# A linear-attention and two-MoE kernel: weight conversions at other places, early weights four chunks ahead, first-step splits moved

## The chip, the core and the metric

One core of one Trainium2 chip. The metric is the device time of one execution in microseconds, median of several runs; the kernel before takes 1228.31 us.

## The reference

The input is attention data (4 batches, 8 heads, 576 positions, head size 64), the probabilities of four experts, and the weights of two feed-forward layers:

```python
q_s = softmax(q, over the 64 columns);  k_s = softmax(k, over the 576 positions)
x = q_s @ (k_s^T @ v)                       # per head; reshaped to 2304 x 512
p = domain_probs / sum(domain_probs)
out = sum over e of p[:, e] * (relu(x @ w1[e]) @ w2[e])     # 4 experts, 512 -> 1024 -> 512
h = out @ w_in;  g = where(h > 0, h, exp(min(h, 0)) - 1)    # 512 -> 2048
return g @ w_out                                            # 2048 -> 512
```

`w_in` and `w_out` come as 64-bit floats; all else is 32-bit.

## The kernel before

**Numbers as pairs.** Each matrix product is done in a fast 32-bit format with a high and a low part: ACT copies the high part, VectorE or GpSimd subtracts it to get the low part, and TensorE does three matmuls (high-high, high-low, low-high). "Splitting" below is that copy and that subtraction.

**Stages.** First comes attention for the sixteen head pairs; the first four (`NPAIR`) are worked off in an order written out by hand (`START`), the others are woven into the next stage. Then comes unit 0, the first expert, in plain form: eight weight chunks `f` (`FPU`), over eight blocks of tokens. `wload` (L403) loads a chunk of both layers into one of two staging buffers `r`, `whi` (L410) and `wlo` (L418) split it; in the first block `wadvance` (L482) splits chunk f+2 after chunk f's first layer, and `wlo_ahead` (L487) starts the next load, since the staging buffer is free then. At the start two chunks are loaded (L527 and `early_loads`, L530).

The rest runs in 30 steps (`STEPS`): ten groups `s` of four chunks by three blocks `b` of 768 tokens. Each step multiplies its first layer with a Strassen scheme: seven products per pair of chunks, two pairs, 14 products (`product`, L1111 is its matmul), with sums in PSUM by VectorE (L1320, L1327) and copies by ACT (L1313, L1315). Steps of s below 5 (`S_FAST`), 15 of them, are "fast": their second layer is a Strassen scheme too (`second_product`, L1255), run during the next step; the intermediate values go through the tile `gt`. In later steps the second layer is plain (`chunk`, L1168 to L1170). Groups s = 0 to 5 belong to experts 2 to 4, s = 6 to 9 (`S_MOE` = 6) to the last layer pair, whose activation needs three ACT functions and two VectorE instructions (`elu`, L1141 to L1146) and a GpSimd subtraction (L1151). Between them the result of the experts is transposed and stored (`turn_steps`, L910 to L965).

**Weights of a step.** `w1_steps` (L714) makes the Strassen sums and splits of the first layer: `sums1` (L746, two subtractions and additions on VectorE, L748 and L749), `sums2` on GpSimd (L753, L754), and splits in between (L733, L744). `w2_fast` (L784) does the same for the second layer of a fast step: `w2_parts` (L769) splits on ACT (L773) and GpSimd (L774), `w2_sum` (L777) is a VectorE subtraction in place (L782).

**Conversions.** No engine computes in 64 bits, so `convert_load` (L428) loads 128 x 512 values of `w_in` or `w_out` as pairs of words (512 KB), `convert` (L440) puts a 32-bit float together in seven instructions (VectorE L455, L461, L465, ACT L468, VectorE L471, L474, and a store to DRAM on SyncE, L477). There are 32 of them, `s // 2` the chunk, `s % 2` the layer; `w_load` (L692) reads the results back from `scratch`. An "aside" conversion uses `gt` for its input and its result (result `y` is L452's slice); the others use the small tiles `ek` and `y`. The result is written first by L461.

**What sets the order.** Each engine and each queue does its work in program order; SyncE (SP) issues nearly all DMAs, one after another, and waits at each until its data and its place are ready. Work that is not TensorE's is hung on hooks: `at(n, fn)` in the first part, one hook per 2048 matmul columns; `at2(i, k, fn)` in the steps, 24 (`SH`) hooks per step, which count on through all steps. A step lets its hooks go at the ends of some products, in batches:

```python
PLAIN, MIXED = ({1: 4, 3: 8, 5: 12, 8: 16, 10: 20, 12: 24}, {      # L1282: after product 1 hooks 0-3, ...
    0: 2, 1: 4, 2: 6, 3: 7, 4: 9, 5: 10, 6: 13, 7: 14, 8: 16, 9: 17, 10: 19, 11: 20, 12: 23, 13: 24,
})
```

`MIXED` holds where the step before was fast, `PLAIN` in the first step and after the fast ones (there `chunk` lets one hook go at a time as well). A conversion is given a hook `t`: its load goes out at t - 7, its six instructions at t + 0, 1, 2, 3, 4, 5 and its store at t + 9 (at 0, 2, 4, 6, 10, 12 and 17 in the fast steps and the first three). The table of hooks is `CONV` (L833 to L837): eight asides in unit 0, thirteen in the fast steps 26 hooks apart, three asides at the end of the fast steps (12 hooks apart, `end1` = 360), eight asides from `end2` (432) + 40 on, again 12 apart.

Of the kernel before, what the change touches and what calls it, by code (L numbers as in the profile page):

```python
# [8 lines left out]
F32 = mybir.dt.float32  # L9
# [12 lines left out]
def tile_attention_moe_moe(  # L22
# [13 lines left out]
    nc = tc.nc  # L36
    NP_, CP, NC, P = q.shape
    D, S = P // 2, NC * CP
    NT, DM = out.shape
    E = w1.shape[0]  # L40
    F2 = w_out.shape[0]
    NPAIR = DM // P
    HALF = S // 2
    KD = DM // P
# [37 lines left out]
    S_MOE = (E - 1) * FPU // FS  # L82
# [22 lines left out]
    stg = ctx.enter_context(tc.tile_pool(name="stg", bufs=2))  # L105
    hp_ = ctx.enter_context(tc.tile_pool(name="hp", bufs=1))
    kvp = ctx.enter_context(tc.tile_pool(name="kvp", bufs=1))
    tmp = ctx.enter_context(tc.tile_pool(name="tmp", bufs=1))
# [18 lines left out]
    gt = hp_.tile([P, 4, TB], F32, name="gt")  # L127
# [273 lines left out]
    raw = {}  # L401

    def wload(u, f):  # L403
        a, b_, _ = units[u]
        r = stg.tile([P, 2, DM], F32, tag="r", name="r")
        nc.sync.dma_start(out=r[:, 0, :].rearrange("p (d f) -> p d f", d=KD), in_=a[f])
        nc.sync.dma_start(out=r[:, 1, :], in_=b_[f * P : (f + 1) * P, :])
        raw[u, f] = (r[:, 0, :].rearrange("p (d f) -> p d f", d=KD), r[:, 1, :])

    def whi(u, f):  # L410
        r1, r2 = raw[u, f]
# [6 lines left out]
    def wlo(u, f):  # L418
        engines = (nc.gpsimd, nc.vector if u == 0 else nc.gpsimd)
        for t, r, eng in zip((w1t[u, f], w2t[u, f]), raw.pop((u, f)), engines):  # L420
            eng.tensor_tensor(out=t[:, 1], in0=r, in1=t[:, 0].bitcast(F32), op=ALU.subtract)  # L421
# [55 lines left out]
        yield lambda: nc.sync.dma_start(out=scratch[s // 2, :, s % 2, :], in_=t["y"])  # L477

    wseq = [(0, f) for f in range(FPU)]
    wnext = [2]  # L480

    def wadvance(u, f):  # L482

        whi(u, f)
        wlo_ahead(u, f)

    def wlo_ahead(u, f):  # L487
        wlo(u, f)
        if wnext[0] < len(wseq):
            wload(*wseq[wnext[0]])  # L490
            wnext[0] += 1

# [26 lines left out]
    t = bank("o")  # L519
# [10 lines left out]
    def early_loads():  # L530
        load(NPAIR - 1, "v")
        wload(*wseq[1])
        for i in range(NPAIR):
            load(i, "q", NC // 2, NC)


    timed = {}

    def at(n, fn):
        timed.setdefault(n, []).append(fn)  # L540
# [41 lines left out]
    for i in range(NP_):  # L582
        late = i >= NPAIR
        t = K_START[i - NPAIR] if late else HALF_STEP * i
        kt = plan_k(i, t) if late else None
        qt = plan_q(i, t + Q_LATE if late else t, kt["kvlo"] if late else 0)
        done.append(qt["xlo"])
        assert qt["xlo"] <= 24 * (i // NPAIR * S // 256 + (not late)) - 2, (i, qt)
        if late:
            for n, when in kt.items():  # L590
                at(when, lambda fn=K_STEPS[n], i=i: fn(i, in_m))
        for n, fn in Q_STEPS.items():
            at(qt[n], lambda fn=fn, i=i: fn(i, in_m, (0, 1) if i >= NPAIR else (1,)))
        if late:
            if i < NPAIR + 2:
                at(i - NPAIR, lambda i=i: load(i, "knqv" if i == NPAIR else "kqv"))
            if i + 2 < NP_:
                at(kt["kv"], lambda i=i: load(i + 2, "kv"))
            if i + 1 < NP_:
                at(kt["kv"], lambda i=i: load(i + 1, "n"))  # L600
            if i + 2 < NP_:
                at(qt["qturn"], lambda i=i: load(i + 2, "q"))
# [111 lines left out]
    def w1_steps(s, p):  # L714

        r, t = [], []
# [23 lines left out]
        tt = nc.vector.tensor_tensor  # L740
# [4 lines left out]

        def sums1():  # L746
            f1, f2 = r[0][:, 0], r[0][:, 1]
            tt(out=f1[:, :2], in0=f1[:, :2], in1=f2[:, :2], op=ALU.subtract)  # L748
            tt(out=f2[:, :2], in0=f2[:, :2], in1=f2[:, 2:], op=ALU.add)  # L749

# [33 lines left out]
    def w2_fast(i, s, d):  # L784

        for k, fn, op in (
            (8, w2_parts, "B11"), (13, w2_sum, "T1"), (17, w2_parts, "T1"), (18, w2_parts, "B22"), (19, w2_sum, "T3"),
            (21, w2_parts, "B21"), (22, w2_parts, "T3"), (24, w2_sum, "T2"), (26, w2_parts, "T2"), (27, w2_sum, "T4"),
            (30, w2_parts, "T4"),
        ):  # L790
            at2(i, k - d, lambda fn=fn, op=op: fn(s, op))

    def w2_step(s, p):
        r = w2r.pop((s, p))
# [11 lines left out]
    def at2(i, k, fn):  # L806
        timed2.setdefault(i * SH + k, []).append(fn)
# [6 lines left out]
    for b in range(NB):  # L814
        need = min(NP_, -(-2 * TB * (b + 1) // S) * NPAIR)
        t = 66 + 36 * b
# [8 lines left out]
        at(n, fn)  # L825
    at(202, lambda: w_load(0, 0, 1))
    at(203, lambda: w_load(0, 1, 1))
    w2_fast(0, 0, 7)

    NCONV = 2 * F2 // P  # L830
    later = lambda n, fn: at2(0, n, fn)
    end1 = NB * S_FAST * SH
    CONV = [(at, t, 1 + (t < 100), True) for t in (30, 50, 70, 146, 160, 173, 185, 197)]  # L833
    CONV += [(later, 34 + 26 * n, 2, False) for n in range(13)]
    CONV += [(later, end1 + 13 + 12 * n, 1, True) for n in range(3)]
    end2 = NB * S_MOE * SH
    CONV += [(later, end2 + 40 + 12 * n, 1, True) for n in range(NCONV - len(CONV))]  # L837
    for s, (put, t, d, aside) in enumerate(CONV):
        put(t - 7, lambda s=s, x=aside: convert_load(s, x))
        for n, fn in zip((0, 1, 2, 3, 4, 5, 9) if d == 1 else (0, 2, 4, 6, 10, 12, 17), convert(s, aside)):  # L840
            put(t + n, fn)
    for i, (s, b) in enumerate(STEPS):
        more = s + 1 < len(STEPS) // NB
# [119 lines left out]
    for b in range(NB):  # L963
        i = NB * (S_MOE - 1) + b + 1
# [79 lines left out]
    for step in START.split():  # L1044
        n, i = step[:-1], int(step[-1])
# [376 lines left out]
```

## Time and profile before

| | us |
|---|---|
| runs: median (lowest to highest) of 3 | 1228.31 (1226.82 to 1230.87) |
| the profiled execution, its own time | 1231.21 |
| its span, first to last instruction | 1229.4 |
| TensorE busy | 1193.3 (97%) |
| VectorE, ACT, GpSimd busy | 826.9, 635.2, 572.8 (67%, 52%, 47%) |
| mean granted clock, as a share of full | 0.989 |

The profile is one execution. PE is TensorE, DVE is VectorE, POOL is GpSimd, SP is SyncE; L followed by a number is a line of the kernel. A row of a timeline gives the start, the length, the instruction with output, input and shape, and in brackets how long its engine had stood before it and what ended that. A table by stretch gives the busy time of each engine in a window, and the clock that TensorE was granted there.

### The profile page before, as it was taken

The numbers are of one execution on the slowest core, as the hardware profiler recorded it, in microseconds if no ns is written. First come the engines' busy times: TensorE is split into PE (matmuls) and PEld (weight loads), VectorE is DVE, ScalarE is ACT, GpSimd is POOL, SyncE is SP. The second block draws the span as 40 slices with busy tenths as digits, with TensorE's granted clock in tenths as the row PEclk, the third lists the DMA queues.
The fourth block names the chain that finished last, engine by engine and source line by source line (L and its number), as shares of the span: only waits on it lengthen the run. The fifth ranks groups of instructions, "written<-read, shape, count | busy, mean of one in ns | idle before, by whom it ended". The sixth has DMA issues, their size and how long they took to land.

```text
span 1229.4 us, 20602 instructions
## 1 busy us (share of the span) xinstructions
PE 1193.3 (97%) x7336; PEld 1102.6 (90%) x7336; DVE 826.9 (67%) x1426; ACT 635.2 (52%) x1361; POOL 572.8 (47%) x544
## 2 busy tenths in 40 slices
PE   8799999999999999999999998999998999999998
PEld 6688889888999999999999997888897888998997
DVE  6776887645687587687686775566677676456443
ACT  6444544335455455455455442446777655556552
POOL 4522543016467467468467552346535434434221
PEclk7899999999999999999999998999999999999999
DMA  7444666756666666567666666999976675655541
GB/s 221 132 132 145 226 223 219 258 182 215 223 223 240 223 207 231 223 230 254 236 234 251 232 234 209 341 318 313 318 282 216 230 255 185 218 190 171 185 158 77
DMA packets 155174, 272.32 MB, mean 222 GB/s; under 512 B 12864, under 2 KB 77888, under 8 KB 155072
## 3 DMA queue, kind: packets, MB, share of 16 engines
q1 hardware_dynamic: 150464, 262.62, 61.9%
q10 hardware_dynamic: 4608, 8.39, 1.9%
q8 instruction: 58, 0.95, 0.3%
q14 instruction: 44, 0.36, 0.1%
HBM read 224.83 MB, written 46.14 MB: 220 GB/s over the span
## 4 chain that ended last, share of the span: by engine, by line
PE 74%; DVE 11%; DMA 6%; ACT 3%; issue 3%; POOL 1%; SPq 1%; DVEq 0%; ACTq 0%; POOLq 0%
PE o L1255 16%; PE h L1111 14%; PE m L1111 14%; PE o L973 7%; PE h L973 7%; PE o L1170 5%; PE o L1169 5%; PE o L1168 5%; DMA scratch<-gt 2%; PE m L283 1%; PE m L375 1%; DMA r<-in_w_dram 1%; DMA xh<-xs 1%; DMA xs<-stage 1%; DVE r L782 1%
## 5 line engine op out<-in xcount | busy, mean ns | idle before, releaser
L1111 PE MATMUL m<-xh,w1s 128*128 128x384 f32 x840 | 246.7, 339 | 12.8 <-DVE h L1320 7.0
L1111 PE MATMUL h<-xh,w1s 128*128 128x384 f32 x840 | 245.2, 338 | 4.3 <-DVE h L1327 3.0
L1111 PEld LDWEIGHTS m<-xh,w1s 128*128 128x128 f32 x840 | 155.0, 188 | 20.9 <-DVE h L1320 9.7
L1111 PEld LDWEIGHTS h<-xh,w1s 128*128 128x128 f32 x840 | 155.4, 189 | 8.8 <-DVE h L1327 4.6
L1111 PE MATMUL h<-xl,w1s 128*128 128x384 f32 x420 | 141.3, 336 | 0.0
L1111 PE MATMUL m<-xl,w1s 128*128 128x384 f32 x420 | 141.1, 336 | 0.0
L1144 DVE SCALAR_TENSOR_TENSOR extra<-extra,half 128x384 f32<-128x384 f32 x96 | 61.3, 639 | 114.7 <-ACT half L1143 114.6
L973 PE MATMUL o<-w2t,hpa 128*128 128x512 f32 x432 | 118.4, 402 | 0.6 <-DVE hpa L1005 0.3
L973 PE MATMUL h<-xh,w1t 128*128 128x256 f32 (+1 forms) x512 | 112.3, 298 | 0.1
L973 PEld LDWEIGHTS h<-xh,w1t 128*128 128x128 f32 x512 | 86.2, 192 | 5.2 <-POOL w1t L421 0.3
L1255 PE MATMUL o<-w2g,xh 128*128 128x256 f32 x540 | 90.4, 282 | 0.0
L973 PEld LDWEIGHTS o<-w2t,hpa 128*128 128x128 f32 x432 | 76.1, 190 | 14.5 <-DVE hpa L1005 1.8
L1255 PE MATMUL o<-w2g,hpa 128*128 128x256 f32 x540 | 88.9, 282 | 0.0
L1255 PE MATMUL o<-w2g,xl 128*128 128x256 f32 x540 | 87.3, 282 | 0.0
L1111 PEld LDWEIGHTS h<-xl,w1s 128*128 128x128 f32 x420 | 79.5, 189 | 1.5
L1111 PEld LDWEIGHTS m<-xl,w1s 128*128 128x128 f32 x420 | 79.2, 189 | 1.5
L1255 PEld LDWEIGHTS o<-w2g,xh 128*128 128x128 f32 x540 | 78.1, 190 | 0.0
L973 PE MATMUL h<-xl,w1t 128*128 128x256 f32 (+1 forms) x256 | 77.5, 303 | 0.0
L1255 PEld LDWEIGHTS o<-w2g,hpa 128*128 128x128 f32 x540 | 76.2, 190 | 0.0
L1255 PEld LDWEIGHTS o<-w2g,xl 128*128 128x128 f32 x540 | 75.8, 190 | 0.0
L1004 ACT ACTIVATE hpa<-h 128x256 fp32r<-128x256 f32 (+1 forms) x64 | 26.0, 406 | 70.9 <-PE h L973 70.8
L744 DVE TENSOR_TENSOR w1s<-r,w1s 128x512 fp32r<-128x512 f32 (+1 forms) x60 | 54.5, 908 | 10.8 <-ACT w1s L733 10.8
(264 smaller groups left out, 2932.5 us busy)
## 6 DMA issues: line engine op xcount, KB each, us to landing
xh<-xs SPq DMA_DIRECT2D x210, 384.0 KB, 5.4
xl<-xs SPq DMA_DIRECT2D x210, 384.0 KB, 6.1
r<-in_w_dram SPq DMA_DIRECT2D x60, 256.0 KB, 4.6
xs<-stage SPq DMA_DIRECT2D x43, 256.0 KB, 3.5
xs<-xh SPq DMA_DIRECT2D x21, 384.0 KB, 4.0
xs<-xl SPq DMA_DIRECT2D x21, 384.0 KB, 4.2
r<-scratch ACTq DMA_DIRECT2D x28, 256.0 KB, 6.2
gt<-in_w_out_dram SPq DMA_DIRECT2D x10, 512.0 KB, 5.0
```

The costliest lines, as they stand in the source:

```text
L283: nc.tensor.matmul(o, ek[:n, ks], vs, start=(c == 0), stop=(c == len(k_chunks) - 1))
L375: nc.tensor.matmul(t[:, a, :HALF], kv[:, l, :], r[:, a, :], start=(n == 0), stop=(n == 2))
L744: eng.tensor_tensor(out=dst(k, 1), in0=src(k), in1=dst(k, 0).bitcast(F32), op=ALU.subtract)
L782: nc.vector.tensor_tensor(out=o, in0=x, in1=y, op=ALU.subtract)
L973: nc.tensor.matmul(out, lhsT, rhs, **kw)
L1004: nc.scalar.activation(out=gh, in_=h, func=AF.Relu)
L1111: nc.tensor.matmul(dst, t[:, wl, c + dl, :], x[xl_][:, dl, :], start=(n == 0 and p < 2), stop=(n == 5), skip_group_check=True,)
L1144: nc.vector.scalar_tensor_tensor(out=e_, in0=e_, scalar=1.0, in1=t, op0=ALU.add, op1=ALU.mult)
L1168: nc.tensor.matmul(o, gh, w[:, 0, :], start=(f == 0), stop=False)
L1169: nc.tensor.matmul(o, gh, w[:, 1, :], start=False, stop=False)
L1170: nc.tensor.matmul(o, gl, w[:, 0, :], start=False, stop=(f == FS - 1))
L1255: nc.tensor.matmul(o, l, r, start=(first_write and m == 0 and c != 1), stop=(m == 5), skip_group_check=True)
```

## The change

- **Early weights.** `wload` puts chunks 2 and 6 of unit 0 into the tile `gt`, which is idle at that time, and chunk 3 into the small tiles `qh` and `ql`; the two staging buffers hold 0, 1, 4, 5 and 7. Chunks 2 and 3 are loaded in `early_loads`, behind the second halves of the queries. The loads then run four chunks ahead (`wnext` begins at 4; after the splits of chunk 3 none is started). Pair 5's attention loads go out at hook 4 instead of hook 1.
- **Conversions.** 8 in unit 0 as before, 16 in the fast steps 21 hooks apart, 2 asides at end1 + 11 and + 25, 6 asides at end2 + 42, 84, 98, 112, 126 and 158. The stores go out at t + 7 instead of t + 9, and at t + 14 instead of t + 17, with L471 and L474 one hook earlier there. The last six are done in the order 27, 29, 31, 26, 28, 30.
- **Second-layer splits of the first step.** `w2_fast` of step 0 comes three hooks earlier; what falls before the step goes to the first part's hooks, 208 for the first split.
- **Sums.** `sums1` runs on GpSimd for s of 6 and more.

```diff
--- before.py
+++ after.py
@@ -402,10 +402,17 @@
 
     def wload(u, f):
         a, b_, _ = units[u]
-        r = stg.tile([P, 2, DM], F32, tag="r", name="r")
-        nc.sync.dma_start(out=r[:, 0, :].rearrange("p (d f) -> p d f", d=KD), in_=a[f])
-        nc.sync.dma_start(out=r[:, 1, :], in_=b_[f * P : (f + 1) * P, :])
-        raw[u, f] = (r[:, 0, :].rearrange("p (d f) -> p d f", d=KD), r[:, 1, :])
+        if f % 4 == 2:
+            r = gt.rearrange("p k n -> p (k n)")[:, : 2 * DM]
+            r = [r[:, :DM], r[:, DM:]]
+        elif f == 3:
+            r = [tmp.tile([P, DM], F32, tag=tag, name="r") for tag in ("qh", "ql")]
+        else:
+            r = stg.tile([P, 2, DM], F32, tag="r", name="r")
+            r = [r[:, 0, :], r[:, 1, :]]
+        nc.sync.dma_start(out=r[0].rearrange("p (d f) -> p d f", d=KD), in_=a[f])
+        nc.sync.dma_start(out=r[1], in_=b_[f * P : (f + 1) * P, :])
+        raw[u, f] = (r[0].rearrange("p (d f) -> p d f", d=KD), r[1])
 
     def whi(u, f):
         r1, r2 = raw[u, f]
@@ -477,7 +484,7 @@
         yield lambda: nc.sync.dma_start(out=scratch[s // 2, :, s % 2, :], in_=t["y"])
 
     wseq = [(0, f) for f in range(FPU)]
-    wnext = [2]
+    wnext = [4]
 
     def wadvance(u, f):
 
@@ -486,7 +493,7 @@
 
     def wlo_ahead(u, f):
         wlo(u, f)
-        if wnext[0] < len(wseq):
+        if f != 3 and wnext[0] < len(wseq):
             wload(*wseq[wnext[0]])
             wnext[0] += 1
 
@@ -532,6 +539,8 @@
         wload(*wseq[1])
         for i in range(NPAIR):
             load(i, "q", NC // 2, NC)
+        wload(*wseq[2])
+        wload(*wseq[3])
 
 
     timed = {}
@@ -593,7 +602,7 @@
             at(qt[n], lambda fn=fn, i=i: fn(i, in_m, (0, 1) if i >= NPAIR else (1,)))
         if late:
             if i < NPAIR + 2:
-                at(i - NPAIR, lambda i=i: load(i, "knqv" if i == NPAIR else "kqv"))
+                at(4 * (i - NPAIR), lambda i=i: load(i, "knqv" if i == NPAIR else "kqv"))
             if i + 2 < NP_:
                 at(kt["kv"], lambda i=i: load(i + 2, "kv"))
             if i + 1 < NP_:
@@ -745,6 +754,7 @@
 
         def sums1():
             f1, f2 = r[0][:, 0], r[0][:, 1]
+            tt = (nc.gpsimd if s >= S_MOE else nc.vector).tensor_tensor
             tt(out=f1[:, :2], in0=f1[:, :2], in1=f2[:, :2], op=ALU.subtract)
             tt(out=f2[:, :2], in0=f2[:, :2], in1=f2[:, 2:], op=ALU.add)
 
@@ -788,7 +798,8 @@
             (21, w2_parts, "B21"), (22, w2_parts, "T3"), (24, w2_sum, "T2"), (26, w2_parts, "T2"), (27, w2_sum, "T4"),
             (30, w2_parts, "T4"),
         ):
-            at2(i, k - d, lambda fn=fn, op=op: fn(s, op))
+            put = lambda k, fn: at2(i, k, fn) if k >= 0 else at(210 + k, fn)
+            put(k - d, lambda fn=fn, op=op: fn(s, op))
 
     def w2_step(s, p):
         r = w2r.pop((s, p))
@@ -825,19 +836,19 @@
         at(n, fn)
     at(202, lambda: w_load(0, 0, 1))
     at(203, lambda: w_load(0, 1, 1))
-    w2_fast(0, 0, 7)
+    w2_fast(0, 0, 10)
 
     NCONV = 2 * F2 // P
     later = lambda n, fn: at2(0, n, fn)
     end1 = NB * S_FAST * SH
     CONV = [(at, t, 1 + (t < 100), True) for t in (30, 50, 70, 146, 160, 173, 185, 197)]
-    CONV += [(later, 34 + 26 * n, 2, False) for n in range(13)]
-    CONV += [(later, end1 + 13 + 12 * n, 1, True) for n in range(3)]
+    CONV += [(later, 34 + 21 * n, 2, False) for n in range(16)]
+    CONV += [(later, end1 + 11, 1, True), (later, end1 + 25, 1, True)]
     end2 = NB * S_MOE * SH
-    CONV += [(later, end2 + 40 + 12 * n, 1, True) for n in range(NCONV - len(CONV))]
-    for s, (put, t, d, aside) in enumerate(CONV):
+    CONV += [(later, end2 + n, 1, True) for n in (42, 84, 98, 112, 126, 158)]
+    for s, (put, t, d, aside) in zip([*range(26), 27, 29, 31, 26, 28, 30], CONV):
         put(t - 7, lambda s=s, x=aside: convert_load(s, x))
-        for n, fn in zip((0, 1, 2, 3, 4, 5, 9) if d == 1 else (0, 2, 4, 6, 10, 12, 17), convert(s, aside)):
+        for n, fn in zip((0, 1, 2, 3, 4, 5, 7) if d == 1 else (0, 2, 4, 6, 9, 11, 14), convert(s, aside)):
             put(t + n, fn)
     for i, (s, b) in enumerate(STEPS):
         more = s + 1 < len(STEPS) // NB
```

## Rows read from the trace of the kernel before

**Rows 1.** Page, part 1: busy us (share of the span) xinstructions.
```profile
PE 1193.3 (97%) x7336; PEld 1102.6 (90%) x7336; DVE 826.9 (67%) x1426; ACT 635.2 (52%) x1361; POOL 572.8 (47%) x544
```

**Rows 2.** By stretch: us, busy us (instructions) per engine, PEclk, DMA, GB/s.
```profile
310.00:728.00 418.00, 415.98 (x2936) 413.93 (x2935) 309.96 (x536) 213.74 (x457) 257.80 (x240) 1.00 0.65 232
...
860.00:1010.00 150.00, 143.84 (x707) 127.01 (x708) 105.12 (x160) 100.27 (x216) 66.81 (x61) 1.00 0.72 256
...
1010.00:1190.00 180.00, 180.00 (x897) 161.74 (x896) 101.88 (x169) 102.27 (x225) 65.35 (x63) 1.00 0.55 196
```

**Rows 3.** TensorE's timeline, 20 to 62: start, us, instruction, [idle before].
```profile
34.65 0.47 PE L352 MATMUL m<-ident,accA 96*128 96x96 f32 x3 [2.44 <-POOL accA L345]
...
41.07 0.67 PE L375 MATMUL m<-hpa,kvs 128*128 128x288 f32 x3 [1.34 <-DVE hpa L367]
...
46.15 0.60 PE L352 MATMUL m<-ident,accA 96*128 96x96 f32 x3 [3.49 <-POOL accA L328]
```

**Rows 4.** Timeline of SyncE, ACT, VectorE and GpSimd in the same stretch.
```profile
21.73 0.35 SPq L406 DMA_DIRECT2D r<-in_w_dram  x1
...
37.65 0.63 ACT L414 ACTIVATE w1t<-r 128x512 fp32r<-128x512 f32 x1 [2.69 <-DMA r<-in_w_dram]
...
44.56 0.54 DVE L322 TENSOR_REDUCE accB<-accA 96x6 f32<-96x384 f32 x1
...
45.18 0.82 POOL L328 TENSOR_TENSOR accA<-accA,accB 96x384 f32<-96x384 f32 x1 [1.09 <-DVE accB L322]
```

**Rows 5.** Table by stretch, for the clock after two waits.
```profile
46.00:50.00 4.00, 3.85 (x32) 3.47 (x33) 3.23 (x7) 2.37 (x7) 2.30 (x2) 0.57 0.54 198
...
756.90:763.10 6.20, 6.20 (x18) 5.72 (x19) 2.83 (x5) 0.87 (x2) 0.00 (x0) 0.50 0.66 217
```

**Rows 6.** Timeline of the first Strassen step: GpSimd, TensorE, VectorE, ACT.
```profile
272.93 1.29 POOL L774 TENSOR_TENSOR w2g<-r,w2g 128x512 fp32r<-128x512 f32 x1 [11.53 <-ACT w2g L773]
...
276.83 0.44 PE L1111 MATMUL m<-xh,w1s 128*128 128x384 f32 x1 [0.85 <-DVE h L1320]
...
293.91 1.50 DVE L782 TENSOR_TENSOR r<-r 128x512 f32<-128x512 f32 x1
...
295.44 0.63 ACT L773 ACTIVATE w2g<-r 128x512 fp32r<-128x512 f32 x1 [2.18 <-DVE r L782]
...
298.08 0.44 PE L1111 MATMUL m<-xh,w1s 128*128 128x384 f32 x1 [1.37 <-ACT h L1315]
```

**Rows 7.** Timeline after the last fast step: SyncE, VectorE, TensorE.
```profile
745.70 0.32 SPq L477 DMA_DIRECT2D scratch<-gt  x1
...
745.74 0.43 DVE L455 TENSOR_SCALAR ce<-gt 128x512 uint16<-128x512 uint16 x1 [1.56 <-DMA gt<-in_w_in_dram]
...
752.83 1.19 DVE L461 TENSOR_SCALAR gt<-gt 128x512 int32<-128x512 int32 x1 [6.67 <-DMA scratch<-gt]
...
756.87 0.69 PE L1111 MATMUL m<-xh,w1s 128*128 128x384 f32 x1 [4.63 <-DVE h L1320]
```

**Rows 8.** TensorE's waits, 860 to 1010: total us, times, longest.
```profile
PE h L1111 <- DVE h L1327: 2.4, 2, 1.9
...
PE m L1111 <- ACT h L1315: 1.2, 1, 1.2
```

**Rows 9.** Line 477, the conversion's store, all of the span.
```profile
DMA to landing us min/median/max: 2.0/4.9/8.4
```

**Rows 10.** Timeline of VectorE and TensorE in the turning stretch.
```profile
816.84 0.96 DVE L748 TENSOR_TENSOR r<-r 128x256 f32<-128x256 f32 x1
...
820.46 0.45 PE L1111 MATMUL m<-xh,w1s 128*128 128x384 f32 x1 [1.18 <-DVE hpa L1120]
```

**Rows 11.** Line 753, sums on GpSimd: duration in ns min/median/max.
```profile
L753 POOL TENSOR_TENSOR r<-r x20: 727/740/852, 256.1 to 1120.4; 128x256 f32<-128x256 f32 x20
```

**Rows 12.** TensorE's waits in the fast steps, 310 to 728 us.
```profile
PE m L1111 <- DVE h L1320: 1.5, 2, 0.9
```

**Rows 13.** Line 748, sums on VectorE: duration in ns min/median/max.
```profile
L748 DVE TENSOR_TENSOR r<-r x20: 410/1040/1400, 254.7 to 1112.3; 128x256 f32<-128x256 f32 x20
```

## The prediction

> **What bounds the kernel now.** I read the busy shares first, then the table by stretch, then what TensorE's own queue waited for, and last the other engines around each wait. TensorE is busy for 97% of the span [rows 1], so the kernel can only gain where TensorE stands still or runs at the lower clock. The table by stretch [rows 2] says where it stands still: 2.0 us in the fast steps (418 less 415.98), 6.2 us between 860 and 1010 us, nothing between 1010 and 1190. So each edit is worth what it takes away from a few single waits, and an engine that gets lighter elsewhere gives nothing.
>
> Three waits lie early [rows 3]: 2.4, 1.3 and 3.5 us. The second and third have one root [rows 4]: ACT waits 2.69 us for the DMA of weight chunk 4, VectorE's split of it starts only then, and VectorE goes without a break from there past L322 at 44.56. The turn at 46.15 is put down to GpSimd's L328, and that one waited for this L322; so whoever is named, the delay is handed on from the DMA. After these waits the granted clock is 0.57 from 46 to 50 us [rows 5]: 3.4 of those 4 us at 1.2 instead of 2.4 GHz, which gives back 1.7 us if the clock stays up.
>
> In the first step two waits, 0.85 and 1.37 us, follow second-layer work [rows 6]: a GpSimd split of 1.29 us stands ahead of first-layer sums, and an ACT split waits 2.18 us for VectorE's sum (1.50 us) from the same batch of hooks while L1315, which TensorE needs, queues behind it.
>
> The largest wait is at 756.87: 4.63 us [rows 7]. VectorE's L461 may not overwrite the conversion's result before the previous store has read it; it stood 6.67 us for that. The store left SyncE at 745.70, just when the load queued ahead of it had landed (VectorE's L455 starts on that load at 745.74). After the wait the clock is 0.50 for 6.2 us [rows 5], which costs another 3.1.
>
> **The change, part by part.** The sum is made against the profiled execution, 1231.2 us, 2.9 above the median of 1228.3.
>
> Weights. Chunks 2 and 3 go to idle buffers, so chunk 4 takes the place in SyncE's queue at 21.73 where chunk 2 stood [rows 4], ahead of pair 4's and pair 5's loads instead of behind them. The four extra issues fall behind the last query loads, where nothing needed is queued behind them; pair 5's loads (with a GpSimd memset) move from hook 1 to hook 4, its first use is hook 12, and chunk 6 waits on SyncE for chunk 2's splits with only those loads behind it. ACT's wait of 2.69 goes, the VectorE run moves by as much, and so does the turn at 46.15: 2.7. Of the 4.8 us of the two waits 2.1 remain; the nearest row to that is a wait of 1.9 us in a stretch that kept clock 1.00 [rows 2, 8], so I add the 1.7 of clock. Gain **4.4**; bounds 1.3 (the second wait alone) and 6.5 (both, and the clock). The first wait of 2.4 stays: chunks 2 and 3 were not late. Next late is VectorE's split of chunk 5.
>
> Second-layer splits of the first step, three hooks earlier. In step 0 hooks run in batches of four. The first split goes before the step, into idle GpSimd time; each sum falls into a batch ahead of its split, except T4's, whose split still moves to the next batch. Gain 0.85 + 1.37 = **2.2**. Bound on the other side: T2's and T4's sums now stand where T3's and T2's stood, and T3's is new in the third batch, ahead of L1207. One sum of 1.5 us in front of a needed instruction costs at most that, so -1.5 to 2.2.
>
> Conversions by the step boundary. With 14 hooks between conversions and the store 7 hooks in, the store precedes the next load, and the next write is 8 hooks off instead of 4. A fast step holds 210 matmuls; 2936 in 418 us [rows 2] makes 14 steps, 1.24 us a hook, so 8 hooks are 9.9 us. Stores land in 4.9 median, 8.4 at most [rows 9]. The wait goes: 4.63 + 3.1 = **7.7**. The third conversion there leaves. Next late would be the load for L455, which stood 1.56 us [rows 7]. Bounds 3.9 (half) and 7.7.
>
> Sums to GpSimd. At 820.46 TensorE waits 1.18 for VectorE's L1120, which stands behind L748 (0.96 us) and its sister L749 [rows 10]. Those two leave VectorE; GpSimd takes 0.74 each [rows 11] behind its own differences. Gain **1.2**; bounds 1.2 and -1.5 (two such instructions ahead of a needed difference).
>
> Conversions from 860 to 1010: the waits on L1327, 2.4 us in two (L461 waiting for the store ahead of them), and the 1.2 on L1315, with a conversion and two sums before it [rows 8]. Six conversions replace eight, stores lead by 8 hooks or more, and for 42 hooks around the first-layer splits, where the wait on L1315 is, there is none. Gain **3.6**; bounds 0 and the whole 6.2 of that stretch [rows 2]. The last conversion moves past 1010, where TensorE never stood; its store is 17 hooks ahead of the load that reads it.
>
> Fast steps: 16 conversions instead of 13. VectorE is 74% busy there (309.96 of 418) and the 13 go with 2.0 us of waits, 0.15 each, so **-0.4**; bounds 0 and -2.8 (three of the worst, 0.9 [rows 12]).
>
> Sum: 4.4 + 2.2 + 7.7 + 1.2 + 3.6 - 0.4 = 18.7. From the profile 1212.5, from the median 1209.6; I take **1211**, since part of the 2.9 may be the very waits that go.
>
> **Rivals.** *The load takes the store's place* (0.12). It is now queued behind the store on SyncE, seven hooks before its use. L461 to L1320 need some 3 us, so it decides if the load lands over 3.7 us later than today's 745.7, after 749.4. For: L455 waits already. Against: the store takes the slot of the load in the queue, not more. Half of the 7.7 and the 2.4 at L1327 stay: 18.7 - 3.9 - 2.4 = 12.4, about 1217.
>
> *GpSimd and VectorE hold each other up* (0.15). L748 takes 0.96 beside GpSimd work at 817 us, though its fastest is 0.41 [rows 10, 13]. If the moved sums hold VectorE as long as they ran on it, the 1.18 at 820 stays: 17.5, about 1212. The Trainium skill (Perfetto Trace Analysis, "Optimizing Scalar/DVE Operations") speaks for this: the two share a read port into the on-chip memory, so that moving work between them "might not help". By that rule the term of 1.2 would be nothing. [...]
>
> *Early weights do nothing* (0.06), that is, the change doesn't do what it says: chunk 4's buffer still frees at 21.7, and if the load or GpSimd's queue ends the wait, the 4.4 is gone: 14.3, about 1215.
>
> *Slower* (0.05). The fast steps: VectorE at 74% gets three more conversions, which now shift by three hooks per step through first-layer splits and second-layer sums. Today's cost is 0.15 each. The other terms give 19.1; if each of 16 cost 1.3 us (19.1 + 2.0 over 16) all would be eaten, and at 1.6 the median would be about 1233. For: L1320 waits there already. Against: the worst such wait is 0.9.
>
> **How the numbers follow.** The forecast has 0.62. All bounds at their good end give 23.8, hence 1204; the upper end, 1220, is 9 above the forecast, which takes in the load rival (6.3) and the lower bounds of any two terms (at most 3.8 + 3.7 = 7.5). About 0.85 lies inside. 0.3% (3.7 us) is what a measurement can tell from no change; below 1224.6 is faster. All cases but the slower one are faster; I take 0.05 from them for bounds that go wrong together: faster 0.90, same 0.05, slower 0.05.
>
> **What would show it.** Right: SyncE's issue of chunk 4 near 22 us and no DMA wait of ACT at L414; the turn of pair 1 near 43; no wait over 0.5 at the two places of the first step (a shorter third between them may stay); L461 without a wait for the store, no lower clock after the step boundary, a span near 1210; L748 on GpSimd from the later experts on. Wrong: L455 waiting for its load at the boundary with TensorE idle behind it, waits on L1320 over 0.9 in the fast steps, or a low clock at 46 us still.

## The result and the profile after

The changed kernel takes 1215.37 us (median of 6 runs, 1213.96 to 1217.34), the kernel before in the same series 1227.57 (6 runs, 1223.04 to 1230.87). The ratio is 0.9904 with a 95% interval of 0.9882 to 0.9925: faster, by 12.2 us between the medians. The profiled execution of after took 1215.79 (span 1214.0), 15.4 less than the one of before.

The busy shares of after, which answer to [rows 1]:

```profile
PE 1186.5 (98%) x7336; PEld 1098.5 (90%) x7336; DVE 819.2 (67%) x1410; ACT 634.5 (52%) x1361; POOL 590.2 (49%) x560
```

The table by stretch, nearly the same work as in [rows 2] and [rows 5] (columns as there: TensorE's matmuls, its weight loads, VectorE, ACT, GpSimd); 720:790 and 746:752 are the step boundary:

```profile
308.00:720.00 412.00, 407.13 (x2861) 403.57 (x2860) 317.11 (x538) 209.65 (x446) 254.83 (x231) 1.00 0.67 235
720.00:790.00 70.00, 69.73 (x403) 64.44 (x402) 40.58 (x72) 29.56 (x61) 26.98 (x28) 1.00 0.87 295
845.00:995.00 150.00, 147.14 (x733) 131.11 (x732) 90.93 (x144) 101.22 (x220) 74.81 (x71) 1.00 0.72 250
995.00:1175.00 180.00, 180.00 (x899) 162.29 (x898) 99.09 (x168) 103.29 (x227) 69.63 (x68) 1.00 0.56 200
746.00:752.00 6.00, 6.00 (x33) 5.49 (x32) 4.61 (x7) 3.19 (x6) 2.83 (x2) 1.00 0.28 103
```

At the boundary TensorE hardly stands still any more and runs at full clock, and in 845:995 it stands still for 3 us less; but in the fast steps its idle time rose from 2.0 us [rows 2] to 4.87.

Both kernels issue the same 7336 matmuls in the same order, so the n-th of one can be laid on the n-th of the other. How much earlier a matmul starts in after, at the end of each stretch of before, gives a ledger without gaps:

| up to the matmul that started in before at | starts earlier by | gained in the stretch | forecast |
|---|---|---|---|
| 34.65 (nothing changed yet takes effect) | 0.98 | 1.0 | - |
| 143.2 (early weights) | 3.66 | 2.7 | 4.4 |
| 236.0 (rest of unit 0) | 3.18 | -0.5 | 0 |
| 310.0 (first step) | 6.37 | 3.2 | 2.2 |
| 728.0 (fast steps) | 2.04 | **-4.3** | -0.4 |
| 763.0 (boundary) | 9.71 | 7.7 | 7.7 |
| 860.3 (turning stretch) | 10.29 | 0.6 | 1.2 |
| 1010.1 | 15.44 | 5.2 | 3.6 |
| 1189.9 | 15.72 | 0.3 | 0 |

The first row is not the work of the change. In the twelve traces of kernels that hold the early weights, the changed kernel and the experiments below, this matmul starts anywhere from 32.2 to 36.5 us, so the start alone differs by 4.3 us between executions. The 0.5 us lost in the rest of unit 0 do not show in the run with the early weights alone, so they belong to another edit; which one was not tested.

**The early waits.** TensorE's timeline of after, the places of [rows 3]:

```profile
42.39 0.44 PE L352 MATMUL m<-ident,accA 96*128 96x96 f32 x3 [2.31 <-POOL accA L328]
...
48.93 0.67 PE L375 MATMUL m<-hpa,kvs 128*128 128x288 f32 x3 [1.69 <-DVE hpa L367]
```

and SyncE and VectorE there:

```profile
20.81 0.33 SPq L413 DMA_DIRECT2D r<-in_w_dram  x1
...
38.41 2.47 DVE L428 TENSOR_TENSOR w2t<-r,w2t 128x512 fp32r<-128x512 f32 x1
...
45.38 2.22 DVE L428 TENSOR_TENSOR w2t<-gt,w2t 128x512 fp32r<-128x512 f32 x1
```

The turn of pair 1 came from 46.15 [rows 3] to 42.39, and between 40 and 60 us the granted clock is 1.00. But 2.31 us of the wait at the turn are left, and a wait of 1.69 us is new: VectorE's split of chunk 6 (2.22 us), which now comes earlier, stands ahead of L367.

**The fast steps.** VectorE's timeline around the longest new wait, and TensorE's matmul after it:

```profile
471.67 0.84 DVE L792 TENSOR_TENSOR r<-r 128x512 f32<-128x512 f32 x1
472.43 1.50 DVE L478 SCALAR_TENSOR_TENSOR ce<-x,ce 128x512 uint16<-128x512 uint16 x1
473.97 1.39 DVE L481 SCALAR_TENSOR_TENSOR y<-y,ce 128x512 f32<-128x512 f32 x1
475.28 1.49 DVE L792 TENSOR_TENSOR r<-r 128x512 f32<-128x512 f32 x1
476.70 0.55 DVE L1331 TENSOR_TENSOR h<-m,extra 128x384 f32<-128x384 f32 x1
...
477.30 0.44 PE L1122 MATMUL m<-xh,w1s 128*128 128x384 f32 x1 [1.38 <-DVE h L1331]
```

Two steps of a conversion (L478, L481) stand between two second-layer sums (L792), 5.1 us in a row without a pause (471.67 to 476.77), and L1331 (before: L1320), which TensorE waits for, is behind them.

**The boundary.** VectorE's second conversion there in after, the place of [rows 7]:

```profile
742.85 0.43 DVE L462 TENSOR_SCALAR ce<-gt 128x512 uint16<-128x512 uint16 x1 [0.71 <-DMA gt<-in_w_out_dram]
743.19 0.42 DVE L468 TENSOR_SCALAR gt<-gt 128x512 int32<-128x512 int32 x1
```

L468 (before: L461) waits for no store any more. L462 waits 0.71 us for its load, and TensorE not at all.

**The turning stretch.** TensorE, the place of [rows 10]: the 1.18 us became two smaller waits.

```profile
809.53 0.44 PE L1122 MATMUL m<-xh,w1s 128*128 128x384 f32 x1 [0.51 <-DVE hpa L1131]
819.85 0.45 PE L1122 MATMUL m<-xh,w1s 128*128 128x384 f32 x1 [0.49 <-DVE h L1331]
```

### The profile page after: what moved, and what is told of

Its sections match the earlier page's. It is cut to its first block, busy times and chain, and to the rows that moved or that the text cites. A ratio compares the mean times of both kernels' runs of the same rounds, so it can differ in the third digit from the quotient of the medians.

```text
span 1214.0 us, 20603 instructions
## 1 busy us (share of the span) xinstructions
PE 1186.5 (98%) x7336; PEld 1098.5 (90%) x7336; DVE 819.2 (67%) x1410; ACT 634.5 (52%) x1361; POOL 590.2 (49%) x560
## 4 chain that ended last, share of the span: by engine, by line
PE 79%; DVE 11%; ACT 3%; issue 3%; DMA 2%; POOL 2%; SPq 0%; DVEq 0%; POOLq 0%; ACTq 0%
PE m L1122 14%; PE h L1122 14%; PE o L1266 14%; PE h L984 7%; PE o L984 7%; PE o L1181 6%; PE o L1180 6%; PE o L1179 6%; DVE accB L1288 1%; DVE w1s L753 1%; PE m L375 1%; DVE gt L1223 1%; PE m L283 1%; DMA xl<-xs 1%; DVE ce L478 1%
## 5 line engine op out<-in xcount | busy, mean ns | idle before, releaser
L1201 POOL TENSOR_TENSOR xh<-gt,xh 128x384 fp32r<-128x384 f32 x31 | 36.5, 1178 | 46.9 <-ACT xh L1200 46.9
```

What stands on the lines that cost most here:

```text
L1201: nc.gpsimd.tensor_tensor(out=gl, in0=src, in1=gh.bitcast(F32), op=ALU.subtract)
```

## The experiments

The question was the fast steps: 4.3 us lost where 0.4 was forecast. The other terms were taken one by one beside it. Idle below is the length of a stretch less the busy time of TensorE's matmuls in it. The kernel before took 1227.4 to 1230.2 us (medians) in the series that these runs belong to, so times are compared by their ratio to it. The time of a single run says little, since the start alone differs by up to 4.3 us; such runs are read by their stretches, from one matmul to the same matmul of another trace.

**Thirteen conversions again.** Two runs, which differ in how the three freed ones are dealt in the first unit.

```diff
-    CONV = [(at, t, 1 + (t < 100), True) for t in (30, 50, 70, 146, 160, 173, 185, 197)]
-    CONV += [(later, 34 + 21 * n, 2, False) for n in range(16)]
+    CONV = [(at, t, 1 + (t < 90), True) for t in (30, 50, 70, 90, 108, 127, 146, 160, 173, 185, 197)]
+    CONV += [(later, 34 + 26 * n, 2, False) for n in range(13)]     # steps 0, 2, 4, 6, 10, 12, 17
```

> The changed kernel with 13 instead of 16 conversions in the fast steps, at the spacing of before (34 + 26n, steps at 0, 2, 4, 6, 10, 12, 17), and the three others dealt to the first unit at hooks 90, 108 and 127. TensorE is idle 4.87 us in 308:720 of the changed kernel and 2.0 us in 310:728 of the kernel before. Theory (the conversions' places and number in the fast steps cost it): idle falls back to about 2.0 us, nothing is added in 60:236 (0.74 us idle there now), time 1215.4 - 2.9 = 1212.5. Rival, the moved splits of the first step or another edit cost it: idle in the fast steps stays at 4 to 5 us, time 1215. Rival, the first unit has no room: its idle time rises by up to 3 x 1.3 = 3.9 us and the time comes out at 1215 to 1216 with the fast steps mended.

> As the run with thirteen (13 conversions in the fast steps at 34 + 26n with the steps of before), but the three in the first unit at hooks 88, 107 and 126 with two hooks between their steps instead of one. In the run with thirteen TensorE was idle 1.75 us in 308:720 (4.87 in the changed kernel) and 5.04 us in 60:236 (0.74), with waits of 1.70 us at 153 and 1.79 us at 179 right behind L478 and L481 of the added conversions, which stood in VectorE's queue one behind the other. Theory (a conversion costs what stands behind its two-input steps when they come in a row): idle in 60:236 falls to 0.7 to 2, the fast steps stay at 1.7, time 1212 to 1213.5 on the scale of the changed kernel's 1215.4. Rival, VectorE has no room for three more in the first unit however they are dealt: 60:236 stays at 4 to 5, time 1215.

Thirteen: 1217.58 us, ratio to before 0.9908 (0.9894 to 0.9921), no faster than the change (0.9904). Gentle: 1215.98 us, 0.9882 (0.9869 to 0.9896). By stretch, first thirteen, then gentle:

```profile
60.00:236.00 176.00, 170.96 (x1235) 151.12 (x1234) 141.80 (x252) 77.23 (x164) 61.56 (x51) 0.99 0.63 207
308.00:720.00 412.00, 410.25 (x2897) 408.32 (x2896) 305.92 (x528) 210.21 (x450) 255.97 (x236) 1.00 0.65 232
```

```profile
60.00:236.00 176.00, 172.48 (x1250) 152.20 (x1250) 141.25 (x256) 78.73 (x166) 61.61 (x52) 1.00 0.63 208
308.00:720.00 412.00, 410.01 (x2892) 408.00 (x2890) 305.44 (x528) 209.83 (x448) 254.56 (x236) 1.00 0.65 232
```

The fast steps are mended (idle 1.75 and 1.99 us), so neither the moved splits nor another edit had cost it. But the first unit lost 5.04 and 3.52 us where it had lost 0.74: the rival came nearer, it has less room than VectorE's busy share of 80% there suggests (141.25 of 176). In thirteen the granted clock also fell to 0.50 for 3.4 us behind the first long wait (155.8 to 159.2). What stands ahead of TensorE's longest wait there (1.79 us, at 180.76), on VectorE and then on GpSimd:

```profile
174.81 3.33 DVE L478 SCALAR_TENSOR_TENSOR ce<-gt,ce 128x512 uint16<-128x512 uint16 x1
178.17 2.20 DVE L481 SCALAR_TENSOR_TENSOR gt<-gt,ce 128x512 f32<-128x512 f32 x1
180.29 0.41 DVE L1016 SCALAR_TENSOR_TENSOR hpa<-h,hpa 128x256 fp32r<-128x256 f32 x1
...
175.76 4.06 POOL L655 TENSOR_TENSOR sum<-sum,xl 128x768 f32<-128x768 f32 x2
```

While GpSimd ran two sums, L478 took 3.33 us and L481 2.20 (their fastest is 0.68), and L1016, for which TensorE waits, stood behind both.

**Other places.** Two runs meant to keep the conversions clear of VectorE's weight work.

```diff
-    CONV += [(later, 34 + 21 * n, 2, False) for n in range(16)]
+    CONV += [(later, 96 * c + t, 3, False) for c in range(4) for t in (30, 46, 72, 88)]    # placed: steps 0, 1, 2, 3, 5, 6, 8
+    CONV += [(later, 96 * c + t, 3, False) for c in range(4) for t in (30, 46, 72)]        # twelve: steps 0, 1, 2, 4, 6, 8, 10
```

> The changed kernel with all 16 conversions left in the fast steps, but none on the hooks where VectorE works on weights (0 to 28 and 56 to 70 of every 96): they begin at 30, 46, 72 and 88 of each 96, steps at 0, 1, 2, 3, 5, 6, 8. Theory A, the place is what costs (a conversion's two-input steps in VectorE's queue ahead of a weight step or of an accumulation): idle in the fast steps falls from 4.87 us to 2.0 to 2.5, time about 1212.5 to 1213. Theory B, the number is what costs (3 more conversions at (4.87 - 2.0) / 3 = 0.96 us each, wherever they stand): idle stays at 4.9 us, time 1215.4.

> The changed kernel with 12 conversions in the fast steps at 30, 46 and 72 of each 96 hooks (clear of VectorE's weight work; steps at 0, 1, 2, 4, 6, 8, 10), and four more in the first unit at hooks 90, 104, 118 and 132. Both theories (place and number) put the idle time of the fast steps at about 1.0 us (4 fewer x 0.96 us by the number; no collision by the place) and the time at about 1211.5. If it stays at 2 us or more, the waits there are not the conversions' at all. If the first unit has no room, its idle time (0.74 us in 60:236) rises by up to 4 x 1.3 = 5.2 us.

Placed: 1222.33 us, 0.9945 (0.9932 to 0.9958). Its last conversion, from hook 376, shares its tile for exponents with the aside that begins at 371 and mixes with it, so it writes wrong values for those weights; the instructions and their sizes are the same. Twelve: 1225.55 us, 0.9964 (0.9949 to 0.9979). My period of 96 hooks was wrong, as the next expectation says, so both put conversions on top of the weight work. By stretch, placed, then twelve:

```profile
308.00:720.00 412.00, 405.05 (x2850) 401.91 (x2850) 307.61 (x526) 205.48 (x441) 250.89 (x231) 1.00 0.65 234
```

```profile
60.00:236.00 176.00, 167.42 (x1229) 148.22 (x1229) 143.23 (x256) 76.82 (x164) 61.55 (x52) 0.98 0.60 197
308.00:720.00 412.00, 408.12 (x2885) 406.81 (x2884) 294.97 (x515) 207.13 (x446) 247.12 (x232) 1.00 0.64 228
```

As a miss they are the test of the number: twelve conversions lost 3.88 us in the fast steps, thirteen had lost 1.75. Fewer cost more, so the number is not the price. By the expectation's own words the waits would then not be the conversions' at all; the run dealt below, in which of all the work in the fast steps only conversions moved, decides against that. Twelve's row of VectorE before its longest wait (1.56 us, at 490.57) is the pattern of after again:

```profile
484.27 1.50 DVE L792 TENSOR_TENSOR r<-r 128x512 f32<-128x512 f32 x1
485.69 1.24 DVE L468 TENSOR_SCALAR y<-x 128x512 int32<-128x512 int32 x1
486.97 1.39 DVE L472 SCALAR_TENSOR_TENSOR y<-x,y 128x512 f32<-128x512 uint32 x1
488.28 1.77 DVE L792 TENSOR_TENSOR r<-r 128x512 f32<-128x512 f32 x1
489.97 0.55 DVE L1331 TENSOR_TENSOR h<-m,extra 128x384 f32<-128x384 f32 x1
```

**Dealt by the period of 72.**

```diff
-    CONV = [(at, t, 1 + (t < 100), True) for t in (30, 50, 70, 146, 160, 173, 185, 197)]
-    CONV += [(later, 34 + 21 * n, 2, False) for n in range(16)]
+    CONV = [(at, t, 1 + (t < 140), True) for t in (30, 50, 70, 94, 119, 146, 160, 173, 185, 197)]
+    CONV += [(later, 72 * c + t, d, False) for c in range(5) for t, d in ((2, 3), (28, 4), (43, 5))][1:]
...
+        put(t - (5 if d == 5 else 7), lambda s=s, x=aside: convert_load(s, x))
+        DEALT = (
+            (0, 1, 2, 3, 4, 5, 7), (0, 2, 4, 6, 9, 11, 14),
+            (0, 2, 6, 7, 8, 14, 16), (0, 1, 3, 4, 6, 8, 10), (0, 3, 6, 7, 9, 11, 14),
+        )
```

> The weights' work on VectorE comes round every 72 hooks (three token blocks of 24), not every 96 as the runs placed and twelve took it; so those two did not test what they were meant to. Here 14 conversions stand in the fast steps, in three fixed places of every 72 hooks, each step on a hook without a weight step of VectorE (those are 57, 59, 61, 67, 68, 70, 0, 6, 13, 19, 24 and 27): from 28 (steps at 0, 1, 3, 4, 6, 8, 10), from 43 (0, 3, 6, 7, 9, 11, 14), and from 2 (0, 2, 6, 7, 8, 14, 16); two more are in the first unit at 94 and 119, two hooks apart. Theory, what counts is what a conversion's step stands next to: idle in the fast steps falls below the 1.75 us of thirteen at the old spacing, to 0.5 to 1.5, although there is one conversion more; time 1211 to 1213. Theory, the number counts: 1.75 + 0.96 = 2.7 us. If it rises to 4 or more, the places are no better than those of the change and the reading of the queue is wrong.

1211.45 us (1210.62 to 1212.56), ratio 0.9843 (0.9829 to 0.9856): faster than the change, whose interval lies wholly above. By stretch:

```profile
60.00:236.00 176.00, 173.76 (x1277) 153.74 (x1276) 141.22 (x256) 79.68 (x170) 60.99 (x52) 1.00 0.63 206
308.00:720.00 412.00, 412.00 (x2922) 412.00 (x2921) 307.79 (x535) 212.21 (x454) 259.49 (x239) 1.00 0.67 236
```

With one conversion more than thirteen, the fast steps have no wait at all, and VectorE is as busy (307.79 against 305.92). By the ledger they run 3.9 us faster than in before, though only 2.0 us of idle time were to be seen there. The second number of the row, the weight loads (PEld), tells the rest: busy 412.00 of 412 here, 413.93 of 418 before [rows 2], 403.57 of 412 after. Its idle time of 0, 4.1 and 8.4 us is the price of the conversions' places in this stretch, and 8.4 - 4.1 gives the ledger's 4.3. This holds for every run: from the matmul at 310.0 of before to the one at 728.0 the fast steps took 414.1 us (dealt) to 425.1 us (placed), and less the idle time of the weight loads it is 413.9 to 414.1 us in all thirteen traces. The rows of the matmuls may hide a short stop because they overlap (a 128x384 row is 0.33 us long where the next starts 0.17 us later); that was not tested.

**The two of the first unit to the boundary.** As dealt, but `(30, 50, 70, 146, ...)` in the first unit and `end1 + t` for t in 11, 25, 39, 53.

> As the run dealt (14 conversions in fixed places of every 72 hooks of the fast steps, idle 0.0 us in 308:720), but the two that had gone to the first unit, where they cost 1.5 us of idle time (2.24 against 0.74), stand behind the two at the boundary, at hooks 39 and 53 of that step, 14 hooks apart like the others. Theory: the first unit is back at 0.74, the boundary has room (VectorE is 58% busy in 720:790, no wait of 0.3 us there), time 1.5 us under dealt: ratio to before about 0.983, 1210 us. Rival, four in a row collide at the boundary with the first layer's sums: waits of 0.5 to 2 us in 760:810, time as dealt or up to 1 us over.

1212.41 us, 0.9871 (0.9851 to 0.9891): no gain over dealt. The first unit is back (idle 0.72), the fast steps stay at 0.0, but the boundary was idle for 3.4 where dealt and after have 0.27:

```profile
720.00:790.00 70.00, 66.63 (x368) 60.30 (x367) 44.55 (x77) 29.00 (x58) 23.11 (x22) 1.00 0.91 307
```

The rival came true, at up to 1.7 us a wait. Hook 53's steps run into the first-layer splits at 57 and beyond, the error of place once more. Dealt keeps the lowest ratio, though the two intervals touch.

**Early weights alone**, the edits of `wload`, `wnext`, `wlo_ahead`, `early_loads` and pair 5's loads put into the kernel before.

> The kernel before with the early weights alone (chunks 2 and 3 loaded at the start into gt and two temporaries, the later loads two chunks further ahead, pair 5's loads at hook 4). Theory from the two traces: 2.4 to 2.7 us faster (1.34 us of the wait at 41 and the 3.49 us at 46 go, the low clock at 43 to 51 goes, and a new wait of 1.7 us on the split of chunk 6 on VectorE comes at 47). Rival, the forecast's own sum: 4.4 us faster, and what was lost of it in the changed kernel was lost to another edit. Rival, early weights do nothing: 0, TensorE waits as long for hpa and hpb.

1226.55 us, ratio 0.9978 (0.9967 to 0.999): 2.7 us (1.2 to 4.1). The early term is 2.7, neither 0 nor 4.4. The time came as expected, but not by the waits that were named:

```profile
42.83 0.44 PE L352 MATMUL m<-ident,accA 96*128 96x96 f32 x3 [3.48 <-POOL accA L328]
...
49.24 0.66 PE L375 MATMUL m<-hpa,kvs 128*128 128x288 f32 x3 [0.34 <-DVE hpa L367]
```

```profile
43.50:46.90 3.40, 3.40 (x29) 2.84 (x28) 2.95 (x8) 2.36 (x6) 2.87 (x4) 0.50 0.00 0
```

Between 30 and 60 us before has two stretches of 3.4 us in which the granted clock is 0.50 (36.0 to 39.5 and 46.3 to 49.7). Every run with the early weights has one, which is worth 1.7 us. In seven of these twelve traces, after among them, it lies ahead of pair 1's turn (34.9 to 38.3 in after), and the waits are about 2.3 and 1.7 us; in the other five it lies behind the turn, and the waits are about 3.5 and 0.35. From the matmul at 34.65 of before to the one at 143.2 both ways take 105.7 to 105.9 us, before 108.5.

This run also holds the boundary of before, unchanged, in another execution; TensorE's wait there, and by stretch the clock after it:

```profile
752.30 0.45 PE L1120 MATMUL m<-xh,w1s 128*128 128x384 f32 x1 [3.40 <-DVE h L1329]
```

```profile
752.30:758.50 6.20, 6.20 (x23) 5.61 (x24) 3.56 (x5) 0.87 (x2) 1.19 (x1) 0.72 0.54 168
```

The same place cost 4.63 us at clock 0.50 in the profiled execution of before [rows 5, 7], and by the ledger 2.4 us more than here. So the profile that I counted in had caught a costlier boundary than this one; two executions do not say which is usual.

**The first step's splits back**, `w2_fast(0, 0, 7)`.

> The changed kernel with the second-layer splits of the first step back where they were (the shift 7 instead of 10). If the first step's gain is theirs, the waits of before return (0.85, 0.58 and 1.37 us at 273, 287 and 295 of before): idle in 236:308 rises from 0.46 us to 2.8 to 3.0, time + 2.4. Rival, the earlier weights had shifted this stretch and the waits are gone anyway: idle stays at 0.5. Whether the fast steps lose less with the splits back (the shift pushes work into their beginning) shows in 308:720: 4.87 us if the shift has no part in it, 2.0 if it is the cause.

1218.82 us in one run. The waits of [rows 6] are back, the first two here, idle in 236:308 is 2.89 us, in 308:720 4.37:

```profile
272.87 0.45 PE L1122 MATMUL m<-xh,w1s 128*128 128x384 f32 x1 [0.86 <-DVE h L1331]
286.77 0.44 PE L1122 MATMUL h<-xh,w1s 128*128 128x384 f32 x1 [0.59 <-DVE h L1338]
```

From the matmul at 236.0 of before to the one at 310.0 it takes 74.0 us as before does, and after 70.8. So the term is theirs, 3.2 us, of which TensorE's idle time shows 2.4; and they have no part in the fast steps, which still lose 4.1 against before.

**The boundary's store.** In the first run it goes out two hooks later, behind the next load; in the second the two conversions stand also 12 instead of 14 hooks apart.

```diff
-        for n, fn in zip((0, 1, 2, 3, 4, 5, 7) if d == 1 else (0, 2, 4, 6, 9, 11, 14), convert(s, aside)):
+        for n, fn in zip((0, 1, 2, 3, 4, 5, 9) if d == 1 else (0, 2, 4, 6, 9, 11, 14), convert(s, aside)):
...
-    CONV += [(later, end1 + 11, 1, True), (later, end1 + 25, 1, True)]
+    CONV += [(later, end1 + 11, 1, True), (later, end1 + 23, 1, True)]
```

> The changed kernel with the aside stores back at hook 9 of their conversion instead of 7, so behind the next one's load and 6 hooks instead of 8 ahead of the next write into the same part of gt. The 4 hooks of before gave a wait of 6.67 us on VectorE at 752.83 and 4.63 us on TensorE; the landings took 2.0 to 8.4 us. Theory, the lead of the store over the next write is what counts: some 2 hooks of 1.1 us come back, a wait of 0 to 2.5 us on L468 at the boundary and 0 to 2 us on TensorE. Rival, the store's place behind the load is what counts: most of the 4.63 us comes back. Rival, the conversions' distance of 14 hooks does it all: 0.

> The changed kernel with the two conversions at the boundary 12 hooks apart instead of 14 and their stores at hook 9 instead of 7: the store stands 4 hooks ahead of the next write into its part of gt, as in the kernel before, but there are two conversions here and not three. With 6 hooks (the run with stores at 9 and a distance of 14) nothing was lost. Theory, the lead is what counts: VectorE waits some 3 to 7 us on L468 around 745 to 755 for the store's landing, and TensorE 2 to 4.7 us; the time rises by that. Rival, the third conversion in a row was the cause of the wait of before (the later stores landed later): VectorE's wait is under 1.5 us and TensorE loses nothing.

1213.53 us and 1217.24 in one run each. VectorE at the boundary with 6 hooks of lead, then VectorE and TensorE with 4:

```profile
745.64 0.43 DVE L468 TENSOR_SCALAR gt<-gt 128x512 int32<-128x512 int32 x1 [5.14 <-DMA scratch<-gt]
```

```profile
746.63 0.43 DVE L468 TENSOR_SCALAR gt<-gt 128x512 int32<-128x512 int32 x1 [5.54 <-DMA scratch<-gt]
...
750.68 0.45 PE L1122 MATMUL m<-xh,w1s 128*128 128x384 f32 x1 [1.86 <-DVE h L1331]
```

VectorE waited for the store in both, 5.14 and 5.54 us, the first twice as long as the expectation's upper end. TensorE lost nothing in the first (idle 0.27 us in 720:790, as in after) and 1.86 us in the second. So the length of VectorE's wait is not its price; what stands behind it is. The store's place behind the load does not cost by itself; two hooks less between the conversions do. They shorten the lead and give the second conversion other neighbours as well, and these runs do not separate the two. With two conversions, 4 hooks of lead give back 1.86 us at full clock, not 4.63; what the third conversion adds was not tried alone.

**The sums back on VectorE**, `tt = nc.vector.tensor_tensor` in `sums1`.

> The changed kernel with the first layer's sums of the last steps back on VectorE. Theory, what the two traces show (0.5 to 0.9 us in the turning stretch): the wait of 0.49 us at 819 becomes one of about 1.2 us, idle in 790:845 rises from 1.35 to 1.9 to 2.3 us and nothing else changes, time + 0.5 to 1. Rival, GpSimd and VectorE hold each other up: without the sums on GpSimd the two-input steps beside them shorten, idle in 790:995 falls, time - 0.5 or better.

1218.26 us in one run, of which 2.5 come from a later start (the matmul of pair 1's turn begins at 44.90, in after at 42.39). TensorE in the turning stretch and later:

```profile
811.58 0.44 PE L1122 MATMUL m<-xh,w1s 128*128 128x384 f32 x1 [1.19 <-DVE hpa L1131]
...
994.44 0.45 PE L1122 MATMUL h<-xh,w1s 128*128 128x384 f32 x1 [0.85 <-ACT m L1326]
```

The wait of [rows 10] is back (1.19 us for its 1.18), the one of 0.49 is gone, and one of 0.85 is new at 994. Idle in 790:845 rises from 1.35 to 1.54, in 845:995 from 2.86 to 3.70. By matmul starts the turning stretch is as long as in after (96.99 and 97.01 us), the stretch from the matmul at 860 of before to the one at 1010 is 1.1 us longer, and the next, to 1190, 0.3. So the sums are worth 1.4 us, all of it later than I had looked.

## Why the prediction was right, and where not

The forecast was 1211 us, 1204 to 1220, faster; measured were 1215.4. The sum of the steps was 18.7 us against 15.4 between the two profiled executions and 12.2 between the medians. The 3.2 between the last two lie mostly in before: its profiled execution was 3.6 us over the median of the six runs. The ledger's 15.7 hold 1.0 from the start, where the change does nothing, and 2.4 by which the boundary of this one execution was costlier than in the early-weights run; without them 12.3 are left. I had taken about half of 2.9 off for this; all of it (1212.5) would have been nearer. That the total is only 4 us off is partly luck: the first step and the stretch from 860 on gave 2.8 more than their terms, while the early weights, the rest of unit 0, the fast steps and the turning stretch gave 6.8 less.

**Fast steps, the step that failed.** The prediction has "the 13 go with 2.0 us of waits, 0.15 each", so -0.4 for three more, with bounds 0 and -2.8. Measured -4.3, beyond the bound. Three things were wrong in it. A price per conversion: twelve cost 3.88 us, fourteen nothing. The base: the 2.0 us of TensorE's idle time was half of what the places cost; the weight loads' idle time of 4.1 stood in the same row [rows 2]. And the bound: I counted the three added ones at the worst wait seen, but a new spacing gives all sixteen new neighbours. The rival *Slower* named the mechanism (conversions shifting through the weight work) and asked 1.3 us of each; by the weight loads' idle time it was 8.4 over 16, 0.5 each.

**Weights.** 4.4 forecast, 2.7 in the ledger, 2.7 alone. The clock gave back its 1.7, one of two stretches of 3.4 us at the low clock. Of the 2.7 of waits only 1.0 came. The turn did move by 2.8, but the next late work took back 1.6 of it: I named the split of chunk 5, which left 2.31 us, but not that of chunk 6, whose 2.22 us now stand ahead of L367. *Early weights do nothing* is ruled out by the run alone.

**First step.** 2.2 forecast, 3.2 in the ledger and by the run that undoes it. The wait between the two, 0.58 us, went as well, and a new one of 0.46 came; the remaining 0.7 do not show in TensorE's idle time (2.92 us before, 0.46 after), but in that of its weight loads (11.2 and 8.0).

**Boundary.** 7.7 forecast and measured in the two profiles, and the signs (no store wait, no lower clock) came as named. Against the execution of the early-weights run the same boundary is worth 5.2, so the exact number rests on the profile that it was counted in. The reason given was too simple: the wait of VectorE could come back without cost. *The load takes the store's place* did not happen: L462 waited 0.71 us for its load.

**Sums.** 1.2 forecast, 1.4 by the run that undoes it, but the number is luck. The wait of 1.18 us went down to 0.51, one of 0.49 came behind it, and by its end the turning stretch had gained nothing by the sums; the 1.4 came after 860 us, where no wait had been counted for them. *GpSimd and VectorE hold each other up* is refuted in its forecast that the 1.18 stays. The Trainium skill (Perfetto Trace Analysis, "Optimizing Scalar/DVE Operations") says such a move may not help, as the two engines share a port; here it helped by 1.4 us. Elsewhere the trace agrees with it: L478 took 3.33 us beside GpSimd's sums. That the port is the cause no run here shows.

**860 to 1010.** 3.6 forecast, 5.2 in the ledger, 4.05 of it in the run with the sums back on VectorE, so that much is the conversions' and 1.1 the sums'. The waits named are gone: the matmuls of before at 923.9 (1.19 us), at 952.4 (1.92) and on to 1008 wait no more, and smaller ones came earlier and between them (0.78, 0.54 and 0.53 us). TensorE's idle time fell by 2.85 us in that run (5.90 to 3.05), so 1.2 are again delay that it does not show.

## What to carry to other kernels

Background work on an engine that is not the bottleneck is priced by its neighbours: list the hooks of the work that TensorE waits for over one full period (here 72 hooks, not a step's 24), and put each step of the background work between them. Thirteen conversions cost 4.1 us at one set of places, sixteen 8.4 at another, and fourteen nothing at a third. Before adding up single waits, take one more execution of the kernel before: here a wait and the low clock behind it cost 2.4 us more in one execution than in another.

## What was not expected of the hardware

TensorE's idle time understated the loss where its weight loads were the tighter row: 2.0 us idle, 4.1 us of idle weight loads, 3.9 us gained when both went to zero. VectorE's L478 (before: L471) took 0.68 to 0.69 us in all 143 cases of the thirteen traces with no GpSimd instruction beside it, and up to 3.72 us with one. It is not only instructions with two inputs: L462 and L468 (before: L455 and L461), which have one, took 0.41 to 0.43 us without and up to 2.07 us with one. And the same start-up code ran in two ways, with waits of 2.31 and 1.69 us (after) or with 3.48 and 0.34 us (early weights alone). They go with the place of the low clock, ahead of the turn or behind it; why it falls here or there was not found out.
